# One more order of all steps on every queue of a linear-attention kernel chained with a GELU MLP

## The chip, the core and the metric

The kernel runs on one core of a Trainium2 chip. A core has a matrix engine (PE, with its weight loads shown apart as PEld), a vector engine (DVE), a scalar engine (ACT), a general engine (POOL) and a queue processor that issues transfers (SP). Each engine takes its own instructions strictly in order and waits for others by semaphores. The metric is the device time of one launch in microseconds (us); lower is better.

## The reference

The first part is a recurrent linear attention (RWKV7) with batch 4, 8 heads, 768 time steps and head size 40. For each head a 40 x 40 state is carried through time:

```python
for t in range(S):
    y[:, :, t] = np.einsum('bhd,bhde->bhe', rt, state)
    Sa = np.einsum('bhde,bhe->bhd', state, at)
    state_decay = state * wt[:, :, None, :] - np.einsum('bhd,bhe->bhde', Sa, bt)
    state = state_decay + np.einsum('bhd,bhe->bhde', vt, kt)
```

Its output, as 3072 tokens of 320 values, goes through an MLP with exact GELU:

```python
x = attn_out.transpose(0, 2, 1, 3).reshape(B * S, H * D)
h = x @ w_in                                     # 320 -> 2048
g = 0.5 * h * (1.0 + erf(h * inv_sqrt2))
return (g @ w_out).astype(np.float32)            # 2048 -> 320
```

All inputs are float32 except the two MLP weights, which come as float64 and are brought to float32 on the chip.

## The kernel before

The time axis is cut into 12 chunks of 64 steps. Inside a chunk the recurrence becomes a set of small matrix products with decays, plus the inverse of a triangular 64 x 64 matrix per head and batch; only the 40 x 40 state passes from chunk to chunk. When a chunk's output is there, its 256 tokens go through the MLP while later chunks are worked on.

The whole program is a list of 1450 small steps, written out as text in `order()` and run one after the other by `perform()`. A token such as `mh.1.0` calls the step `mh` with the numbers 1 and 0. The first number is the chunk for nearly all steps. Engines run what they are given in the order in which the tokens stand, so the text is the order of every queue. There is nothing else that decides it: no planner runs. Results of PE go to four PSUM banks, handed out round robin as they become idle (`take`, `drop`).

The steps that the following text names, with the engine in brackets:

- Loads (SP): `Lw`, `La`, `Lb`, `Lk`, `Lr`, `LV`, `Lv`, `Lwt`, `Lbt`, `Lkt` bring the inputs of one chunk; `Lf`, `Lf5` (L537) bring pieces of w_in and `Ls` (L577) of w_out.
- Conversion of the float64 weights: `ce`, `cn`, `cl` (ACT), `cs`, `cm`, `cv` (DVE) and `cg` (POOL, L658), in 18 units.
- Fillers (PE): `warm_first` and `warm.4.i` are matmuls whose result nobody uses. `warm_set` and `Tt_zero` are memsets.
- Decays: `lg` (ACT, a logarithm, L685), `wT` and `cu` (PE, products with a triangle of ones), `ew`, `ec` (ACT, L742); from chunk 3 on `tw` (PE), `lt` (ACT, logarithm), `pw`, `en`.
- Transposes: `ta`, `tb`, `tk`, `tr`, `tv` (PE), each followed by a scaled copy: `sa`, `sb` (DVE, L784), `sn`, `kc`, `rc`, `vc` (ACT).
- Products and masks: `nm` (PE), `nk` (DVE, L864); `am`, `ak`; `vm`, `vk`.
- The triangular inverse: for chunk 0 on PE and DVE (`qt`, `qi`, `qm` on PE, `qz` L1036, `qb` L1045, `qa`, `qc`, `ql`, `qx`); for the others on POOL (`ic.c.j0.j1`, L961 and L963), between `iz`, `nd`, `nx` (L927) and `wx`, `wa`, `wb`, `tc_`, `jm`, `jc`, `km`, `kt0`, `kt1`.
- Output and state: `av`, `xm`, `sm`, `pk`, `pb` (PE), `ym` (PE) and `yc` (ACT), `sc` (DVE, two passes of L1175, masks), `xc0`, `xc1`, `oa` and `om` (DVE, L1227, L1233), `od`, `oc`, `ot`, `tn`. `om` writes the tokens into `xt`.
- `ox.c.x` (SP, L1245 and L1248) moves part of `xt` to other partitions of SBUF by transfers, eleven for a chunk. The MLP's first product needs them.
- The MLP: `mh.c.p` (PE, L1307, 20 matmul records in 64x128 tiles), `ge.c.q` (ACT, GELU, L1312, for two `mh` each), then the second product in seven products of quarter size, `m1` to `m7` (PE, L1346), with the sums `s1` to `s4` before them and `e1` to `e6` after them (DVE L1299, ACT). Chunk 0 has a plain second product `pm.0.n` (PE, L1428) with copies `pc`. `so` and `sz` (SP) write the output.

ACT holds one set of function tables at a time; logarithm, exponential and GELU need different ones, so a change among them brings a table load.

Of the kernel before, what the change touches and what calls it, by code (L numbers as in the profile page):

```python
# [18 lines left out]
def order(chunks, first_seven):  # L19
    return """  # L20
        first_ones.1 Lw.1 stripes_set identity pads_extra.1 sums_mask Lw.0 pads_r.1 warm.4.20 upper_mask
        pads_extra.3 La.0 pads_a.1 warm.4.0 pads_VR.1 pads_VR.0 of_half_set Lb.0 bias_set warm.4.13 pads_r.0 lg.1
# [13 lines left out]
        mh.0.0 nk.2 ot.0.1 cg.6 ot.0.0 ak.1 Ls.1 nd.2 Ls.0 nx.2 mh.0.1 iz.2 ce.8 tn.0 LV.2 unused.a mh.0.2 wb.1
        cs.8 ic.2.0.4 Lk.2 cm.8 cv.8 ge.0.0 av.1 Ls.6 ce.11 ym.1 ce.10 cs.11 ic.2.4.8 Ls.5 mh.0.3 tc_.1 Lr.2
        cm.11 yc.1 sk.2.v xm.1 cs.10 Ls.7 ge.0.1 cm.10 tv.2 ic.2.8.12 Ls.9 xc1.1 cv.10 xc0.1 Ls.10 jm.1 vc.2
        cv.11 Ls.8 tr.2 ce.12 tk.2 Ls.11 mh.0.6 ce.13 cs.12 ic.2.12.16 La.3 cm.12 kc.2 cs.13 mh.0.7 wa.1.1 cm.13
        jc.1 cv.12 rc.2 am.2 vm.2 cv.13 ic.2.16.20 ce.14 pm.0.0 Ls.13 cl.14 cs.14 Ls.12 ce.15 cm.14 ak.2 Lw.3  # L40
# [5 lines left out]
        La.4 sa.3 wa.2.1 kt1.2 wa.2.0 nm.3 kt0.2 so.0.0 sm.2 nk.3 Lkt.3 mh.1.1 nd.3 sc.2.0 nx.3 lg.4 Lv.3 pk.2
        sc.2.1 ic.3.0.4 pb.2 ge.1.0 tk.3 mh.1.6 ic.3.4.8 oa.2.0 Lr.4 ta.4 mh.1.7 ws.0 LV.3 ws.1 mh.1.4 ge.1.3
        Lbt.4 ic.3.8.12 tr.4 mh.1.5 oa.2.1 Lk.4 kc.3 mh.1.2 tv.3 od.2.0 Lwt.4 ic.3.12.16 mh.1.3 od.2.1 oc.2
        om.2.0 vm.3 Lb.3 ge.1.1 am.3 ge.1.2 vk.3 m1.1 ot.2.1 ic.3.16.20 s1.1 ot.2.0 om.2.1 m2.1 s2.1 ox.2.1 ak.3
        m5.1 e1.1 tn.2 ws.3 av.3 e3.1 ic.3.20.24 s3.1 Lkt.4 ym.3 e2.1 tw.4 m6.1 yc.3 s4.1 ox.2.0 m3.1 ws.2 lt.4  # L50
        tk.4 m7.1 ic.3.24.28 e4.1 LV.4 tb.4 m4.1 e5.1 Lr.5 ic.3.28.31 xm.3 e6.1 pw.4 so.1.1 mh.2.6 xc0.3 La.5
        wx.3 ew.4 tc_.3 cu.4 sb.3 jm.3 en.4 so.1.0 mh.2.7 wb.3 sn.4 Lv.4 wa.3.0 jc.3 xc1.3 wa.3.1 km.3 sa.4 ec.4
        mh.2.4 sk.4.p tr.5 ge.2.3 kt1.3 Lkt.5 iz.4 ta.5 kt0.3 nm.4 sm.3 nk.4 Lw.5 mh.2.5 nd.4 nx.4 sc.3.0
        ic.4.0.4 mh.2.2 sc.3.1 Lbt.5 tv.4 mh.2.3 ic.4.4.8 kc.4 Lb.4 pk.3 ge.2.1 Lwt.5 ge.2.2 tb.5 pb.3 mh.2.0
        ic.4.8.12 sb.4 oa.3.1 oa.3.0 mh.2.1 od.3.0 om.3.1 am.4 ge.2.0 ic.4.12.16 om.3.0 vm.4 od.3.1 ox.3.1 m1.2
        s1.2 lg.5 tw.5 oc.3 ot.3.0 m2.2 s2.2 s4.2 m5.2 Lv.5 e1.2 vk.4 lt.5 ic.4.16.20 ot.3.1 s3.2 m6.2 ox.3.0
        ak.4 pw.5 m3.2 e3.2 ew.5 m7.2 La.6 e2.2 ic.4.20.24 tn.3 en.5 e4.2 m4.2 e5.2 av.4 e6.2 tk.5 so.2.1
        ic.4.24.28 ym.4 sn.5 Lr.6 mh.3.6 yc.4 sa.5 tv.5 LV.5 xm.4 ic.4.28.31 cu.5 xc1.4 xc0.4 mh.3.7 ec.5 wx.4
        tc_.4 wa.4.1 iz.5 ta.6 nm.5 ge.3.3 vm.5 Lbt.6 tr.6 wb.4 jm.4 nk.5 mh.3.2 jc.4 nd.5 Lwt.6 wa.4.0 nx.5
        mh.3.3 kc.5 ic.5.0.4 Lkt.6 vk.5 km.4 ge.3.1 mh.3.0 kt1.4 ic.5.4.8 kt0.4 tb.6 La.7 am.5 sm.4 tw.6  # L60
# [5 lines left out]
        ic.6.0.4 ge.4.3 jm.5 am.6 jc.5 wa.5.1 km.5 wa.5.0 tw.7 sk.5.p mh.4.3 kt0.5 tb.7 ic.6.4.8 kt1.5 La.8
        mh.4.0 ak.6 ge.4.1 sm.5 Lb.6 ic.6.8.12 mh.4.1 sc.5.1 tr.7 pk.5 sc.5.0 ge.4.0 Lkt.7 ic.6.12.16 pb.5 lt.7
        cu.6 oa.5.1 Lw.7 mh.4.4 oa.5.0 pw.7 ic.6.16.20 mh.4.5 LV.7 om.5.1 m1.4 ge.4.2 Lv.7 od.5.0 om.5.0 s1.4
        m2.4 ec.6 ox.5.1 s2.4 ic.6.20.24 m5.4 od.5.1 ew.7 s3.4 en.7 s4.4 m6.4 oc.5 sn.7 ot.5.0 so.3.0 ot.5.1 m3.4
        sa.7 Lk.7 nm.7 e1.4 ox.5.0 ic.6.24.28 e3.4 e2.4 m7.4 e4.4 tn.5 m4.4 e5.4 ic.6.28.31 av.6 e6.4 nk.7 so.4.1  # L70
        sk.6.p ym.6 sb.6 wx.6 mh.5.6 wb.6 tv.7 iz.7 nd.7 tk.7 yc.6 mh.5.7 nx.7 Lr.8 wa.6.1 ic.7.0.4 vm.7 ge.5.3
        xm.6 Lwt.8 vk.7 mh.5.2 ic.7.4.8 xc0.6 ta.8 kc.7 Lbt.8 mh.5.3 xc1.6 tc_.6 tr.8 mh.5.0 ic.7.8.12 ge.5.1
        Lkt.8 tb.8 jm.6 lg.7 am.7 jc.6 Lb.7 wa.6.0 km.6 ic.7.12.16 tw.8 mh.5.1 so.4.0 kt1.6 ak.7 kt0.6 lt.8 Lv.8
        mh.5.4 pw.8 ic.7.16.20 ge.5.0 sm.6 mh.5.5 sc.6.0 sc.6.1 pk.6 ge.5.2 s1.5 pb.6 Lk.8 cu.7 oa.6.1 m1.5 La.9
        om.6.1 oa.6.0 ec.7 m2.5 sk.7.p od.6.0 om.6.0 s2.5 ox.6.1 m5.5 ic.7.20.24 e1.5 od.6.1 s3.5 oc.6 ew.8 m6.5
        s4.5 en.8 e2.5 m3.5 LV.8 e3.5 ot.6.0 e4.5 sa.8 ot.6.1 ox.6.0 m7.5 tn.6 ic.7.24.28 tk.8 m4.5 e5.5 Lr.9
        ic.7.28.31 av.7 e6.5 sb.7 sn.8 ym.7 so.5.1 mh.6.2 yc.7 wx.7 tc_.7 iz.8 Lb.8 xm.7 nm.8 mh.6.3 nk.8 nd.8
        tv.8 mh.6.6 xc1.7 Lwt.9 ge.6.1 nx.8 mh.6.7 kc.8 ic.8.0.4 Lw.8 vm.8 ge.6.3 am.8 xc0.7 vk.8 jm.7 ic.8.4.8
        wa.7.1 tw.9 mh.6.4 ta.9 lt.9 Lv.9 jc.7 pw.9 wb.7 mh.6.0 ic.8.8.12 lg.8 Lbt.9 wa.7.0 km.7 mh.6.1 kt1.7
        ak.8 kt0.7 ic.8.12.16 sm.7 ge.6.0 mh.6.5 sc.7.1 sc.7.0 tb.9 cu.8 ge.6.2 ic.8.16.20 Lw.9 pk.7 s1.6 pb.7  # L80
# [1386 lines left out]
```

## Time and profile before

| | us |
|---|---|
| median of three runs | 639.3 (638.05 to 640.16) |
| the profiled execution, its span | 638.6 |
| PE busy | 621.4 |
| PEld busy | 548.3 |
| DVE busy | 457.9 |
| POOL busy | 380.3 |
| ACT busy | 323.6 |

The profiled execution took its span; no other time lies around it. In the rows of the timeline the first number is the start in us, the second the length of the stretch, then the engine and the line; the tile written stands left of the arrow, the tiles read right of it; x8 counts instructions, and what released the first of them after idle time stands in brackets. "SPq" is the stretch in which SP issues a transfer, not its landing. Rows by windows give the busy time of each engine in that window with the number of instructions, then the clock granted to PE, the share of the DMA engines and GB/s. The chain of waits is followed back from the last instruction; its rows have start, length, engine and line.

### The profile page before, as it was taken

What the parts mean: (1) busy time and instruction counts of PE and PEld (TensorE: products, weight loads), DVE (VectorE), ACT (ScalarE), POOL (GpSimd) and SP (SyncE); (2) the same over time, 40 slices, a digit from 0 to 9 for tenths busy, and PEclk for the clock granted to TensorE, in tenths of its full rate; (3) what the DMA queues carried; (4) which work ended last, traced back from release to release, by engine and by line L of the source; (5) the groups of instructions that cost most, each with busy time, mean ns of one, the idle gap of its engine ahead of it and who ended that gap; (6) DMA issues with size and microseconds to landing.
All of it is one profiled execution on the core that took longest, in us unless ns stands there. A gap on an engine that the chain in (4) does not pass through costs nothing.

```text
span 638.6 us, 27896 instructions
## 1 busy us (share of the span) xinstructions
PE 621.4 (97%) x12418; PEld 548.3 (86%) x12418; DVE 457.9 (72%) x557; ACT 323.6 (51%) x456; POOL 380.3 (60%) x782
## 2 busy tenths in 40 slices
...
PEclk9799999999999999999999999999999999999999
...
GB/s 136 181 162 178 91 178 187 143 104 137 91 135 149 59 98 159 64 147 111 110 84 133 76 93 107 88 88 157 68 92 109 41 37 84 42 26 3 36 7 21
DMA packets 246899, 64.07 MB, mean 100 GB/s; under 512 B 228380, under 2 KB 243644, under 8 KB 246780
## 3 DMA queue, kind: packets, MB, share of 16 engines
...
q14 instruction: 22, 0.18, 0.1%
...
## 4 chain that ended last, share of the span: by engine, by line
PE 76%; ACT 2%; DVE 0%; issue 0%; DVEq 0%
PE bank L1307 30%; PE bank L1346 27%; PE bank L193 19%; ACT Tt L937 0%; ACT SM L1154 0%; ACT L1312 0%; ACT spare L922 0%; DVE spare L864 0%; ACT st L1194 0%; ACT gt L1312 0%; ACT T L942 0%; DVE Tt L932 0%; ACT st L1192 0%; ACT Tt L1116 0%; DVE os L1299 0%
## 5 line engine op out<-in xcount | busy, mean ns | idle before, releaser
L1307 PE MATMUL bank<-xt,w_in_sb 64*128 64x256 f32 x1920 | 221.3, 381 | 0.2 <-ACT gt L1312 0.2
L961 POOL TENSOR_TENSOR tmp<-W,Nb 128x126 f32<-128x126 f32 (+22 forms) x341 | 164.4, 482 | 93.1 <-DVE Nb L927 67.6
L1307 PEld LDWEIGHTS bank<-xt,w_in_sb 64*128 64x128 f32 x1920 | 182.5, 187 | 25.1 <-issue 1.5
L963 POOL TENSOR_TENSOR W<-W,tmp 128x126 f32<-128x126 f32 (+22 forms) x341 | 168.8, 495 | 26.7
L1346 PE MATMUL bank<-w_out_sb,gt 128*128 128x160 f32 x704 | 101.1, 301 | 0.0
L1346 PEld LDWEIGHTS bank<-w_out_sb,gt 128*128 128x128 f32 x704 | 96.6, 190 | 2.2 <-issue 1.2
L1312 ACT ACTIVATE gt<-bank 128x1024 f32<-128x1024 f32 x48 | 48.7, 1024 | 94.9 <-PE bank L1307 94.6
L1175 DVE TENSOR_TENSOR SM<-bank,upper 128x832 f32<-128x832 f32 (+1 forms) x24 | 23.0, 988 | 20.3 <-PE bank L193 20.2
L1263 ACT COPY conv<-st 32x128 f32<-32x128 f32 (+2 forms) x55 | 28.0, 509 | 17.0 <-DVE st L1257 16.2
L1299 DVE TENSOR_TENSOR conv<-gt 128x1024 f32<-128x1024 f32 x11 | 14.2, 1290 | 25.1 <-ACT gt L1312 25.0
L1227 DVE TENSOR_TENSOR st<-bank,st 128x832 f32<-128x832 f32 (+1 forms) x22 | 21.2, 985 | 14.0 <-PE bank L193 14.0
L1346 PE MATMUL bank<-extra,conv 128*128 128x160 f32 x208 | 30.3, 300 | 0.0
L1299 DVE TENSOR_TENSOR os<-os,bank 128x160 f32<-128x160 f32 x44 | 13.8, 315 | 22.1 <-PE bank L1346 20.5
L1346 PEld LDWEIGHTS bank<-extra,conv 128*128 128x128 f32 x208 | 28.9, 190 | 0.1
L721 DVE TENSOR_TENSOR_SCAN kT<-spare,kT 128x256 f32<-128x256 f32 x36 | 26.6, 798 | 0.6 <-ACT kT L714 0.6
L1346 PE MATMUL bank<-extra,gt 128*128 128x160 f32 x176 | 25.8, 300 | 0.0
L1346 PEld LDWEIGHTS bank<-extra,gt 128*128 128x128 f32 x176 | 24.5, 190 | 0.1
L789 POOL TENSOR_TENSOR bk_rows<-bk_rows,part 128x640 f32<-128x640 f32 x9 | 14.3, 1591 | 14.3 <-ACT part L742 13.9
L1312 ACT ACT_TABLE_LOAD x17 | 21.8, 1283 | 0.3
L1346 PE MATMUL bank<-extra,SM 128*128 128x160 f32 x144 | 21.2, 300 | 0.0
L193 PEld LDWEIGHTS bank<-SM,Tt 64*64 64x64 f32 x768 | 17.1, 133 | 4.2 <-issue 2.3
L193 PE MATMUL bank<-SM,Tt 64*64 64x104 f32 (+1 forms) x768 | 19.3, 249 | 0.9 <-ACT Tt L1113 0.9
...
## 6 DMA issues: line engine op xcount, KB each, us to landing
...
```

What stands on the lines that cost most here:

```text
L193: nc.tensor.matmul(o, lhsT, rhs, start=first, stop=True, skip_group_check=True)
L721: nc.vector.tensor_tensor_scan(logs[:, at:at + n], onward, logs[:, at:at + n], 0.0, ALU.mult, ALU.add)
L789: (nc.vector if q == "v" else nc.gpsimd).tensor_tensor(to, rows(k_of(c)), decays(c), ALU.mult)
L961: nc.gpsimd.tensor_tensor(t, W[:, BL // 2 - rows:, rest:rest + 1].to_broadcast([P, rows, rest]), Nb[:, rest:rest + 1, :rest].to_broadcast( ...
L963: nc.gpsimd.tensor_tensor(own, own, t, ALU.add)
L1175: nc.vector.tensor_tensor(SM[:, g, :, :, cols], pair_of(f"S{c}_", g).rearrange("p x i c -> p i x c")[:, :, :, cols], kept, ALU.mult)
L1227: nc.vector.tensor_tensor(to, pair_of(f"QY{c}_", g)[:, :, :, cols], to, ALU.add)
L1263: nc.scalar.copy(apart.rearrange("p e i g d -> p (e i g) d")[to_rows, :, to_col:to_col + n], st.rearrange("p e i g c -> p (e i g) c")[rows ...
L1299: nc.vector.tensor_tensor(to, one_, other, how)
L1307: nc.tensor.matmul(ph[:, x, s], w_in_sb[half(x), kt, p * P:(p + 1) * P], xt[half(x), kt], start=kt == 0, stop=kt == NK - 1)
L1312: nc.scalar.activation(gt[:, 4 * q:4 * q + 4].rearrange("p (x s) t -> p x s t", x=2), bank(f"ph{c}_{q}").rearrange("p x (s t) -> p x s t", ...
L1346: nc.tensor.matmul(po[:, n, :DM // 2], l_[:, f], r_[:, f], start=f == 0, stop=f == NF // 2 - 1)
```

## The change

Only the text in `order()` is changed. The list holds the same 1450 tokens, each as often as before, in another order; after it every line number is smaller by five, since the text is five lines shorter. Instructions, tiles, sizes and buffers are the same, except that the PSUM bank of a product depends on the order, and that table loads of ACT go where the order puts them: 55 of them after, 48 before.

The beginning, before and after (chunk 0's loads and `warm_first` first; chunk 1's steps later):

```diff
-        first_ones.1 Lw.1 stripes_set identity pads_extra.1 sums_mask Lw.0 pads_r.1 warm.4.20 upper_mask
-        pads_extra.3 La.0 pads_a.1 warm.4.0 pads_VR.1 pads_VR.0 of_half_set Lb.0 bias_set warm.4.13 pads_r.0 lg.1
-        first_ones.0 pads_w.0 pads_rows.0 warm.4.25 pads_extra.0 Lb.1 pads_rows.1 onward_set lg.0 pads_w.1 wT.1
-        pads_a.0 pads_extra.2 La.1 wT.0 warm.4.2 ew.1 Lf.0.1.0 ta.0 Lf.1.1.0 cu.0 Lf.0.0.0 cu.1 ec.0 Lf.1.0.0
-        ew.0 sb.0 tb.0 sa.0 Lk.0 warm.4.15 sn.0 ec.1 nm.0 sb.1 Lf.2.0.0 warm_set tb.1 nk.0 Lf5.0.0 ta.1 sn.1 qt
-        parity_set iz.1 sa.1 qm.0 qi.0.p qi.1.v nm.1 qz.0 warm_first ce.1 Lf.3.0.0 nk.1 qb.0.0.v Lf.3.1.0 qc.0
-        cs.1 qb.0.1.a nd.1 qm.1 sk.0.p ce.0 nx.1 Lr.0 cm.1 Tt_zero tk.0 cs.0 cn.1 ic.1.0.4 qc.1 Lf.2.1.0 cl.1
...
+        Lw.0 pads_a.1 warm_set pads_a.0 Tt_zero identity bias_set pads_VR.1 warm_first sums_mask warm.4.25 La.0 Lb.0
+        pads_extra.3 lg.0 of_half_set pads_w.0 warm.4.13 wT.0 upper_mask first_ones.0 cu.0 pads_extra.0 ec.0 sb.0 ta.0
+        Lw.1 ew.0 sa.0 tb.0 sn.0 nm.0 stripes_set parity_set nk.0 qt warm.4.24 lg.1 Lf.1.0.0 Lf.1.1.0 qi.0.p ce.1 cs.1
+        cm.1 pads_extra.1 cu.1 Lb.1 La.1 qm.0 qz.0 qb.0.0.v ec.1 pads_w.1 wT.1 ew.1 cn.1 sb.1 pads_extra.2 ta.1 tb.1
+        sn.1 first_ones.1 sa.1 qb.0.1.a qc.0 nm.1 qi.1.v qm.1 cl.1 nk.1 Lk.0 Lf.2.1.1 qz.1 qb.1.0.v warm.4.0 Lf.0.0.0
```

From the first `om` to the first `mh`, and around the second `pm` pair:

```diff
-        La.2 tv.1 om.0.1 om.0.0 Ls.2 cs.4 cm.4 Lf.3.0.1 vc.1 tr.1 od.0.1 cv.4 ox.0.0 am.1 rc.1 unused.v wT.2 ce.6
-        sb.2 warm.4.1 one_set od.0.0 wx.1 ew.2 ta.2 ox.0.1 tb.2 sa.2 vm.1 sn.2 cs.6 cl.6 cm.6 nm.2 vk.1 oc.0 cn.6
...
-        cv.16 pk.1 cn.17 cg.17 pb.1 ge.0.2 oa.1.0 cu.3 Lk.3 oa.1.1 pm.0.3 ec.3 od.1.0 Lw.4 ic.2.28.31 od.1.1 oc.1
-        tw.3 ot.1.0 om.1.1 sk.3.p ot.1.1 om.1.0 av.2 tn.1 ox.1.1 pc.0.1 lt.3 ym.2 wx.2 iz.3 pm.0.2 tc_.2 yc.2
...
+        cl.6 od.0.1 vc.1 Lb.2 sb.2 wT.2 oc.0 ot.0.0 warm.4.20 La.2 ta.2 Lk.2 cs.4 cm.4 tb.2 Ls.0 ic.1.24.28 ic.1.28.31
+        ox.0.0 ew.2 cv.4 unused.a sa.2 vm.1 sn.2 Ls.2 Lf.3.1.1 ox.0.1 wx.1 warm.4.4 ce.6 ot.0.1 cs.6 cm.6 cn.6 nm.2
...
+        ce.17 cm.16 ak.2 pk.1 pb.1 lg.3 cs.17 cm.17 cn.17 ic.2.20.24 Lwt.3 mh.0.4 mh.0.5 tw.3 lt.3 Lr.3 oa.1.0 LV.3
+        od.1.0 cv.16 oa.1.1 od.1.1 ge.0.2 Lbt.3 cu.3 cg.17 Lb.3 Lv.3 om.1.1 om.1.0 ox.1.0 ec.3 pm.0.3 av.2 ic.2.24.28
```

One later place, around the products of chunk 4:

```diff
-        kt1.4 ic.5.4.8 kt0.4 tb.6 La.7 am.5 sm.4 tw.6
-        ic.5.8.12 mh.3.1 lt.6 Lk.5 sc.4.1 sc.4.0 Lw.6 ak.5 mh.3.4 ge.3.0 pw.6 ic.5.12.16 mh.3.5 Lv.6 pk.4 ge.3.2
-        s1.3 pb.4 so.2.0 lg.6 av.5 oa.4.1 ic.5.16.20 oa.4.0 m1.3 od.4.1 od.4.0 om.4.0 oc.4 m2.3 om.4.1 ot.4.0
...
+        mh.3.5 wa.4.0 kt0.4 ge.3.2 tr.6 sm.4 sc.4.0 Lkt.6 Lv.6 sc.4.1 pk.4 pb.4 s1.3 oa.4.0 od.4.0 oa.4.1 od.4.1 m1.3
+        oc.4 ot.4.1 s2.3 om.4.1 m2.3 e1.3 ic.5.8.12 m5.3 av.5 ot.4.0 ic.5.12.16 ic.5.16.20 ic.5.20.24 om.4.0 tn.4 ym.5
```

The rest of the list is reordered in the same manner; within the blocks of the MLP the `mh` steps and `m` steps stand in longer runs at some places and in shorter ones at others.

More of the change, by code (lines that the diff above doesn't have):

```diff
@@ L36, in order @@
[L36 to L40, printed above, removed]
@@ L46, in order @@
[L46 to L50, printed above, removed]
@@ L51, in order @@
[L51 to L60, printed above, removed]
@@ L66, in order @@
[L66 to L75, printed above, removed]
@@ L76, in order @@
[L76 to L80, printed above, removed]
@@ new lines, in order @@
+        tb.3 oc.1 ot.1.0 ot.1.1 tn.1 ym.2 pm.0.2 yc.2 ic.2.28.31 pw.3 wx.2 tc_.2 ew.3 sa.3 en.3 jm.2 jc.2 wa.2.0
+        wa.2.1 xm.2 xc0.2 sn.3 unused.r tr.3 ox.1.1 nm.3 nk.3 Lkt.3 pc.0.1 sb.3 mh.1.0 wb.2 nd.3 nx.3 km.2 kt1.2 xc1.2
+        mh.1.1 pc.0.0 kt0.2 sm.2 tv.3 La.4 ge.1.0 sc.2.1 sc.2.0 vm.3 vk.3 tk.3 kc.3 Lr.4 ta.4 Lbt.4 Lk.4 mh.1.2 pk.2
+        pb.2 mh.1.4 mh.1.5 oa.2.1 od.2.1 ge.1.2 mh.1.6 mh.1.7 ge.1.3 oa.2.0 od.2.0 ws.0 ws.1 ws.2 mh.1.3 tr.4 oc.2
+        so.0.0 ot.2.1 am.3 om.2.0 Lk.3 ge.1.1 m1.1 Lw.4 m2.1 ak.3 av.3 ot.2.0 tn.2 ym.3 om.2.1 Lwt.4 ox.2.0 e1.1 s1.1
@@ new lines, in order @@
+        mh.2.1 od.3.0 am.4 om.3.1 Lwt.5 Lr.5 tw.5 so.1.1 so.1.0 La.6 vm.4 om.3.0 ge.2.0 s1.2 s4.2 Lv.5 s2.2 m1.2 m2.2
+        s3.2 m5.2 m6.2 lt.5 iz.4 e1.2 e2.2 m3.2 m7.2 ic.4.0.4 ak.4 m4.2 vk.4 e3.2 ic.4.4.8 ic.4.8.12 ic.4.12.16
+        ic.4.16.20 ic.4.20.24 pw.5 ox.3.1 e4.2 e5.2 oc.3 ot.3.0 ox.3.0 ot.3.1 tn.3 ew.5 Lk.5 e6.2 so.2.1 cu.5 ec.5
+        av.4 en.5 tr.5 ym.4 tv.5 sn.5 mh.3.6 yc.4 mh.3.7 ge.3.3 Lkt.5 sa.5 tk.5 kc.5 ic.4.24.28 xm.4 xc1.4 ta.6 Lw.6
+        xc0.4 nm.5 nk.5 ic.4.28.31 wx.4 tc_.4 nd.5 nx.5 Lwt.6 iz.5 mh.3.2 mh.3.3 ge.3.1 LV.5 ic.5.0.4 am.5 vm.5 mh.3.0
```

104 lines of the change are left out of this document (63 added, 41 removed).

## The prediction

> **What bounds the kernel now.** I read the page's busy times first, then busy time by windows of 20 us, then the chain of waits, then the queues line by line over the first 140 us.
>
> ```profile
> span 638.6 us, 27896 instructions
> PE 621.4 (97%) x12418; PEld 548.3 (86%) x12418; DVE 457.9 (72%) x557; ACT 323.6 (51%) x456; POOL 380.3 (60%) x782
> PE 76%; ACT 2%; DVE 0%; issue 0%; DVEq 0%
> ...
> 20.00:40.00 20.00, 16.99 (x352) 11.77 (x350) 15.82 (x23) 11.39 (x17) 12.78 (x25) 0.83 1.07 167
> 40.00:60.00 20.00, 17.40 (x502) 13.66 (x504) 19.30 (x30) 15.15 (x23) 17.27 (x35) 1.00 0.85 173
> 60.00:80.00 20.00, 19.50 (x542) 16.78 (x544) 17.47 (x30) 15.47 (x22) 6.81 (x14) 1.00 0.59 108
> 120.00:140.00 20.00, 17.12 (x406) 12.89 (x400) 15.08 (x21) 16.94 (x24) 7.49 (x12) 1.00 0.46 89
> ...
> 138.94:635.03 496.09, 495.34 (x9590) 451.29 (x9584) 351.79 (x402) 224.08 (x323) 293.77 (x590) 1.00 0.47 86
> ```
>
> PE works 97% of the span, and 76% of the chain of waits lies on it. In a window columns follow as PE, PEld, DVE, ACT, POOL, then PEclk. From 138.94 us to the last matmul PE is busy for 495.34 of 496.09 us, and no other engine is full. So an order can win there only by removing small stalls or changes of tile form. The holes are in the head: 3.01, 2.60 and 2.88 us in three of the four early windows shown. At 40 to 60 us it is DVE that is full, 19.30 of 20.
>
> **The head.** Part 1, chunk 0's loads and first chain come ahead of chunk 1's.
>
> ```profile
> 0.81 1.48 SPq L447 DMA_DIRECT2D SM<-in_w_dram  x2
> 2.32 1.94 SPq L447 DMA_DIRECT2D w_tile<-in_w_dram  x2
> 2.70 6.26 PE L193 MATMUL bank<-cum_m,ident 128*128 128x512 f32 x8 [2.70 <-POOL cum_m L360]
> 9.87 1.11 PE L193 MATMUL bank<-cum_m,w_tile 64*64 64x64 f32 x64
> 12.75 1.24 PE L193 MATMUL bank<-w_tile,cum_m 128*128 128x320 f32 x4
> 19.72 1.16 DVE L864 TENSOR_TENSOR N<-bank,upper 128x1024 f32<-128x1024 f32 x1
> ```
>
> The two Lw.1 transfers (1.48 us of SP) leave the way of Lw.0, La.0 and Lb.0, and wT.1, ta.0 and a filler leave the way of cu.0 on PE. Four fillers ended at 2.70 + 6.26 = 8.96; now warm_first and two fillers stand there, started by DVE's short memset instead of POOL's cum_m. I let them end near 8.2 (estimate: warm_first's 4.86, row below, from about 1, and half of the 6.26 shortened as the clock rises). wT.0 (1.11) follows, then cu.0 at about 9.3 instead of 12.75. From cu.0 to nk.0 it was 19.72 - 12.75 = 6.97, so nk.0 comes at about 16.3: 3.4 earlier.
>
> Part 2, warm_first leaves the inverse of chunk 0.
>
> ```profile
> 27.69 4.86 PE L193 MATMUL bank<-w_in_sb 128*128 128x512 f32 x6
> 28.97 0.48 DVE L1045 TENSOR_SCALAR st<-st,of_half 128x512 f32<-128x512 f32 x1
> 32.48 2.08 PE L193 MATMUL bank<-turned,st 64*64 64x64 f32 x64
> ...
> 20.88:67.83 46.95, 40.95 (x1066) 31.15 (x1066) 41.72 (x64) 31.75 (x45) 33.40 (x68) 0.93 0.97 169
> ...
> 66.54 1.29 DVE L1233 TENSOR_TENSOR xt<-bank,wpT 128x512 f32<-128x512 f32 x2 [0.15 <-PE bank L193]
> ```
>
> qm.1's last input was there at 28.97 + 0.48 = 29.45, but PE sat in warm_first until 32.5. That is 3.0 more, 6.4 with part 1. ACT takes ec.1 and ew.1 ahead of chunk 0's copies now, so I take 5.6: qm.1 near 26.9. Not all of this lasts. From nk.0's end to om.0's end DVE is busy for 41.72 of 46.95 us, and in the new order it has nearly the same passes there; kc.0 and other copies on ACT stand between too. That gives back about 1.6 (estimate; at worst 5.6, with om.0 where it was, at best nothing). I put om.0 at 66.54 - 4.0.
>
> Part 3, SP's queue.
>
> ```profile
> 64.52 1.33 SPq L577 DMA_DIRECT2D w_out_sb<-in_moe_w_out_dram  x2
> 65.91 0.61 SPq L537 DMA_DIRECT2D gt<-in_moe_w_in_dram  x1
> 67.91 0.90 SPq L1245 DMA_DIRECT2D xt<-xt  x1
> 74.34 3.25 SPq L1248 DMA_DIRECT2D xt<-xt  x4
> 76.58 7.27 PE L1307 MATMUL bank<-xt,w_in_sb 64*128 64x256 f32 x60
> 78.83 4.61 PEld L1307 LDWEIGHTS bank<-xt,w_in_sb 64*128 64x128 f32 x42 [0.23 <-DMA xt<-xt]
> ```
>
> The first MLP product waits for the eleven transfers of ox.0.0 and ox.0.1, which SP issues one after the other from 67.91 to 77.59. After the change Ls.2 (1.33) and Lf.3.1.1 (0.61) stand between the two: 1.9 of the 4.0 are given back. mh.0.0 gains 2.0 to 2.6.
>
> Part 4, from there to mh.1.0, the last piece of the head.
>
> ```profile
> 119.85 1.56 POOL L658 TENSOR_TENSOR conv<-conv,bk_rows 128x640 f32<-128x640 f32 x1 [1.00 <-ACT conv L650]
> 122.16 0.77 PE L193 MATMUL bank<-w_tile,cum_m 64*64 64x320 f32 x8 [1.36 <-ACT gt L1312]
> 122.86 4.58 PE L1428 MATMUL bank<-w_out_sb,gt 128*128 128x320 f32 x16
> 138.25 0.22 PE L193 MATMUL bank<-Tt,Js 32*32 32x32 f32 x2 [1.52 <-ACT Js L1091]
> 138.94 2.43 PE L1307 MATMUL bank<-xt,w_in_sb 64*128 64x256 f32 x20
> ```
>
> Stalls of 1.36 and 1.52 stand here, and both go: the instructions in front are others. New ones come. ge.0.2 on ACT stands behind lt.3, so behind tw.3 on PE and the load Lwt.3 on SP; and on SP, Lb.3 waits for POOL's cg.17 (at 119.85), with Lv.3, ox.1.0 and ox.1.1 queued behind it. pm.0.3, which needs ge.0.2, may then stand still for up to 3 us, and jm.2 and nm.3 for some tenths. nm.3 comes before mh.1.0 now and km.2 after it, which I let cancel. Bounds for mh.1.0's gain: 2.6 + 1.36 + 1.52 = 5.5 with no new stall; 2.0 + 2.9 - 3.0 - 1.0 = 0.9 with all of them. I take half of a 2.6 us stall: 2.3 + 2.9 - 1.3 = 3.9.
>
> **The steady part.** The same 1450 steps are issued, so PE's matmuls are the same. What can differ is the changes between tile forms and stalls.
>
> ```profile
> 184.46 2.36 PE bank L1307 x20
> 602.15 17.47 PE bank L1307 x160
> ```
>
> A single mh step (20 matmuls) takes 2.36; eight in a row 17.47/8 = 2.18. One interruption costs 0.18, or less where the neighbour has another form. Counted over both PE queues from mh.1.0 on there are 130 runs of one form before, 135 after; weighed by form this adds 0.66 us (bounds: 0, and 5 x 0.2 = 1.0).
>
> ```profile
> 435.01 1.66 PE L193 MATMUL bank<-SM,Tt 64*64 64x104 f32 x64
> 436.49 0.72 PE L193 MATMUL bank<-w_tile,cum_m 64*64 64x320 f32 x8
> 436.63 1.02 DVE L1175 TENSOR_TENSOR SM<-bank,upper 128x832 f32<-128x832 f32 x1 [1.85 <-PE bank L193]
> 465.76 0.32 DVE L1299 TENSOR_TENSOR os<-os,bank 128x160 f32<-128x160 f32 x1
> ```
>
> The kernel of before keeps small work between a product and the step that reads its mask. pb needs both sc passes of 1.02 behind sm, 2.04 and a handover (0.1, as an estimate). In chunks 4 and 10 the new order has sm, pk, pb adjacent, so only pk's 1.66 lies in front: 2.04 + 0.1 - 1.66, about 0.5 each. av.7 and av.8 stand behind the passes of e5 (0.32 each) with two short steps between, 0.3 each; m1.1 behind ge.1.1 (1.02), 0.45; ym.10 and mh.9.4 0.5 together; the rest, by the same subtraction, 0.9 (all estimates). Sum 3.5. In before the window above shows 0.75 of open idle time, and PE takes 2.2 more than its matmuls at the rates of unbroken runs, such as 2.18 above; I count the 2.2. So +1.3; bounds -2.2, with no stall at all, and +5, if each handover is 0.2 longer in some 20 places.
>
> ACT loads its function tables 55 times instead of 48.
>
> ```profile
> L1312 ACT ACT_TABLE_LOAD x17 | 21.8, 1283 | 0.3
> L1312 ACT ACTIVATE gt<-bank 128x1024 f32<-128x1024 f32 x48 | 48.7, 1024 | 94.9 <-PE bank L1307 94.6
> ```
>
> Seven more are 7 x 1.28 = 9.0 us of an engine that is busy half the time. I take 0, since ge, which releases PSUM banks, waited 94.6 us for PE and not the other way; the bound is 9.0, all on the path. [...]
>
> **The tail.** e5.11, its output, e6.11 and the last output stay in that order; 0.
>
> ```profile
> 635.07 0.32 DVE L1299 TENSOR_TENSOR os<-os,bank 128x160 f32<-128x160 f32 x1 [0.91 <-PE bank L1346]
> ```
>
> **Sum.** 638.6 - 3.9 + 0.66 + 1.3 = 636.7 for a profiled execution. The profile of before lies 0.7 under the median of its runs (639.3; 638.05 to 640.16), hence 637.4 less rounding: I forecast 637.3.
>
> **The rivals.** *The head's gain stays whole.* If ge.0.2 and ox.1 come in time, mh.1.0 gains 5.5, and if the tight places cost no more than before the steady part adds 0.66: 639.3 - 4.8 = 634.5. For it: the stalls at 122.16 and 138.25 are real and their cause is gone. Against: SP's order gives back 1.9 in sight, and the sums at pb.4 and pb.10 leave little room.
>
> *Slower: Gelu behind a table switch.* The new order puts ge.0.2, ge.2.2, ge.2.0, ge.4.1, ge.6.1, ge.7.3 and ge.8.0 directly behind a switch, after steps that themselves wait for PE (lt, lg, ec). There are four PSUM banks, so a late ge holds its bank and PE's next product waits. Each exposed switch costs 1.28, all seven 9.0: 637.4 + 9.0 = 646.4, with four of them 642.5. The change is slower than before from the second exposed one on (1.9/1.28 = 1.5). For it: PE is without a gap, so no delay is absorbed later. Against: ge waits for PE in before by 94.6 us in 48 calls, 2 each.
>
> *No change: the clock.*
>
> ```profile
> PEclk9799999999999999999999999999999999999999
> ```
>
> PEclk is 7 in the second slice and 0.83 at 20 to 40; it fell while PE ran the small tiles of the inverse, and warm_first filled that stretch. If qm.1 to qm.3 now run at half clock, their 2.08 each doubles, plus transposes and products around them: about +6 in the chain up to om.0, the 4.0 are lost and 2 more, while the old stalls of 2.9 still go: 639.3 + 2.0 - 2.9 + 0.66 + 1.3 = 640.4. Against: qm steps are short and DVE is the bound at 40 to 60. [...]
>
> **How the numbers follow.** Small net gain (637.3, own range 635.8 to 639) 0.43; whole gain 0.22; Gelu behind switches 0.25; clock 0.10. Differences under 0.3% (637.4 to 641.2) a measurement of this kernel can't tell from no change. Of the first case a little over half lies below 637.4, all of the second: faster 0.46. The upper end of the third and a few executions of the first lie above 641.2, with unseen stalls of the same kind: slower 0.30. Same 0.24. Range 632.5 to 644: below, the whole gain with the -2.2 of no stalls at all; above, five exposed switches.
>
> **What would show it.** nk.0 at 16 to 17 and qm.1 at 26 to 27.5 show parts 1 and 2; the time between the transfers of ox.0.0 and of ox.0.1 shows part 3; pm.0.3's idle time and mh.1.0 at 134 to 136 show part 4. From mh.1.0 to the last matmul I expect 498.1 instead of 496.1. Idle time of PE put down to "ACT gt L1312" above 3 us would show the slower rival; PEclk under 0.8 at 20 to 40 the clock. The prediction is wrong if PE's idle time after 140 us is far from 3.5 us in total, either way.

## The result, and the profile after

The changed kernel takes 647.7 us (median of 4 executions, 646.4 to 650.1) against 638.9 for the kernel before (4 executions in the same session): ratio 1.0135, 95% interval 1.0103 to 1.0166. It is slower, where a small gain was forecast, and longer than the 632.5 to 644 that the forecast allowed. One correction to the table above: in these runs the time of an execution is its span plus 1.9 us (646.81 for the changed kernel's profiled one, span 644.9). So the profile of before stands for about 640.5, a little above its median and not 0.7 under it. The forecast used the difference only.

Three lines of the changed kernel's page:

```profile
span 644.9 us, 27921 instructions
PE 625.9 (97%) x12418; PEld 551.6 (86%) x12418; DVE 457.7 (71%) x557; ACT 332.5 (52%) x463; POOL 375.0 (58%) x782
PEclk9798989999999999999999999999999999999999
```

and its busy time by windows, columns as before:

```profile
20.00:40.00 20.00, 16.25 (x286) 13.24 (x281) 11.80 (x18) 10.42 (x15) 7.04 (x17) 0.74 0.98 182
40.00:60.00 20.00, 17.84 (x491) 14.36 (x483) 17.56 (x28) 15.07 (x22) 17.41 (x35) 0.91 0.85 160
80.00:100.00 20.00, 19.20 (x384) 16.67 (x384) 14.63 (x23) 14.81 (x20) 16.37 (x37) 0.91 0.89 203
...
141.33:641.28 499.95, 497.05 (x9588) 450.53 (x9584) 350.61 (x403) 232.57 (x329) 289.64 (x593) 1.00 0.47 86
```

The clock falls three times ahead of the last matmul where it fell once: the trace's clock records have half clock from 22.6 to 32.8, 53.3 to 56.7 and 80.6 to 84.0 us (before: 24.95 to 31.78 only). mh.1.0 starts at 141.33 instead of 138.94, 2.4 later where 3.9 earlier was forecast. From there to the last matmul it takes 499.95 instead of 496.09, 3.9 more where 2.0 was forecast. That is the 6.3 us between the two profiles.

The head line by line, first PE, then DVE, then SP:

```profile
18.11 1.42 PE L188 MATMUL bank<-N,st 32*32 32x32 f32 x128 [0.40 <-DVE st L995]
23.19 0.49 PE L188 MATMUL bank<-cum_m,SM 64*64 64x64 f32 x7 [2.65 <-issue]
23.61 1.97 PE L746 MATMUL bank<-ident,spare 128*128 128x128 f32 x8
25.36 1.91 PE L746 MATMUL bank<-ident,extra 128*128 128x128 f32 x8
28.38 1.99 PE L188 MATMUL bank<-aT,nT 40*64 40x64 f32 x64 [1.10 <-DVE turned L1002]
30.14 3.24 PE L188 MATMUL bank<-turned,st 64*64 64x64 f32 x64
51.92 0.57 PE L188 MATMUL bank<-rT,late 40*64 40x64 f32 x21 [1.17 <-issue]
80.80 6.16 PE L1302 MATMUL bank<-xt,w_in_sb 64*128 64x256 f32 x38 [1.70 <-DMA xt<-xt]
126.60 4.54 PE L1423 MATMUL bank<-w_out_sb,gt 128*128 128x320 f32 x16 [0.50 <-issue]
...
15.55 1.23 DVE L859 TENSOR_TENSOR N<-bank,upper 128x1024 f32<-128x1024 f32 x1 [2.02 <-PE bank L188]
68.04 1.27 DVE L1228 TENSOR_TENSOR xt<-bank,wpT 128x512 f32<-128x512 f32 x2
...
69.38 0.91 SPq L1240 DMA_DIRECT2D xt<-xt  x1
73.83 0.91 SPq L572 DMA_DIRECT2D w_out_sb<-in_moe_w_out_dram  x2
74.78 0.78 SPq L532 DMA_DIRECT2D gt<-in_moe_w_in_dram  x2
75.61 1.57 SPq L1240 DMA_DIRECT2D xt<-xt  x2
```

nk.0 (15.55) does come 4.2 us earlier. But PE then stands still for 2.65 us inside wT.1, put down to "issue": nothing in the profile that it waits for. The clock falls there, and ta.1 and tb.1 (1.97 and 1.91, where the old order took 1.04 and 1.09) and most of qm.1 (3.24 instead of 2.08) run at half clock; nm.1 (1.99) did so in the kernel before as well. om.0 (68.04) comes 1.5 later than before, not 4 earlier.

The rows show one thing more. wT.1, ta.1 and tb.1 ran ahead of qm.0 in the old order; now they stand between qm.0 and qm.1, in the place that warm_first has left. With the pause, and the wait at nm.1, PE goes from the end of qm.0 (19.53) to qm.1 in 10.6 us, where it took 6.6. The queue of ACT waits for them, too:

```profile
23.73 1.04 ACT L723 ACTIVATE wpT<-bank 128x1024 f32<-128x1024 f32 x1 [4.08 <-PE bank L188]
27.32 1.01 ACT L796 COPY nT<-bank 128x1024 f32<-128x1024 f32 x1 [2.04 <-PE bank L746]
28.85 0.57 ACT L1026 COPY turned<-bank 128x512 f32<-128x512 f32 x1
```

ew.1 (23.73) waits for wT.1 and sn.1 (27.32) for tb.1, and qc.0 (28.85), the last step that qm.1 needs, stands behind both. It ends at 29.42. In the kernel before, qm.1's last input was there at 29.45. So the whole gain of part 1 is gone before qm.1 begins.

**What the pauses under "issue" are.** The page has a queue "q8 instruction" with 97 transfers, 1.59 MB, so 16 KB each; PE executes 12418 matmuls and as many weight loads, and 1.59 MB over these is 64 bytes each. So I read q8 as PE's stream of instructions: 128 matmul records, with their loads, to a transfer (an estimate from these counts). From the records of the trace, the pauses inside one step of small tiles in four kernels (records counted from the first matmul; us):

```
kernel      step   record  transfer starts, lands   PE goes on   behind the landing
before      qm.0      348      22.25    23.72          25.30          1.58
changed     wT.1      350      20.47    21.56          23.19          1.63
changed     vm.0      858      49.14    50.27          51.92          1.66
h_after     vm.0      858      50.54    52.02          53.62          1.60
fill_three  qm.1      476      28.35    29.31          30.81          1.50
changed     ym.6     6592     326.85   328.24         329.73          1.49
changed     xm.8     8758     430.85   431.88         433.25          1.37
```

In these rows PE goes on 1.4 to 1.7 us behind a landing, and within the head the places lie 126 records (350 to 476) or four times 127 (350 to 858) apart. The transfers of q8 start at least 3.34 us apart in the profile of the kernel before and 3.60 in that of the changed one, while 128 records of small tiles run in 1.4 to 3.3 us (in the changed kernel the 128 of qm.0 in 1.4, 64 of nm.0 in 1.2, 64 of sm.4 in 1.66). So, as I read these numbers, a long run of small tiles uses up its instructions here; no experiment tests that alone. What sets the start of a transfer isn't shown.

Past mh.1.0 the view of PE's waits (total, times, longest), and then two rows of the timeline with the places under "issue":

```profile
PE bank L188 <- issue: 1.3, 2, 0.8
PE bank L1302 <- DVE os L1294: 0.7, 1, 0.7
PE bank L188 <- DVE SM L1170: 0.5, 2, 0.4
```

```profile
329.72 0.91 PE L188 MATMUL bank<-rT,turned 40*64 40x64 f32 x43 [0.49 <-issue]
433.25 0.58 PE L188 MATMUL bank<-st,aT 40*64 40x104 f32 x13 [0.78 <-issue]
```

Against each step's own usual length in these kernels, the largest excesses are xm.8 1.3, mh.2.6 0.9 (the next mh needs a bank that DVE's sums release), ym.6 0.8, pb.4 0.8, pb.10 0.5, ym.10 0.3, av.7 0.2, am.9 0.2. No wait of PE for GELU ("ACT gt") is left.

### The profile page after: what moved, and what is told of

Read it like the earlier page. It is cut to its first block, busy times and chain, and to the rows that moved or that the text cites. A ratio compares the mean times of both kernels' runs of the same rounds, so it can differ in the third digit from the quotient of the medians.

```text
span 644.9 us, 27921 instructions
## 1 busy us (share of the span) xinstructions
PE 625.9 (97%) x12418; PEld 551.6 (86%) x12418; DVE 457.7 (71%) x557; ACT 332.5 (52%) x463; POOL 375.0 (58%) x782
## 3 DMA queue, kind: packets, MB, share of 16 engines
q8 instruction: 97, 1.59, 1.1%
## 4 chain that ended last, share of the span: by engine, by line
PE 91%; DVE 4%; issue 2%; SPq 1%; DMA 1%; ACT 1%; DVEq 0%; ACTq 0%
PE bank L1302 34%; PE bank L188 28%; PE bank L1341 25%; PE bank L1423 3%; DVE SM L1170 1%; PE bank L746 1%; DMA xt<-xt 1%; DVE kT L716 0%; SPq L1243 0%; DVE conv L630 0%; DVE turned L1002 0%; DVE xt L1228 0%; ACT L729 0%; DVE st L995 0%; DVE spare L859 0%
## 5 line engine op out<-in xcount | busy, mean ns | idle before, releaser
L1302 PE MATMUL bank<-xt,w_in_sb 64*128 64x256 f32 x1920 | 224.6, 384 | 2.8 <-DMA xt<-xt 1.7
L956 POOL TENSOR_TENSOR tmp<-W,Nb 128x126 f32<-128x126 f32 (+22 forms) x341 | 165.9, 486 | 74.6 <-DVE Nb L922 49.1
L958 POOL TENSOR_TENSOR W<-W,tmp 128x126 f32<-128x126 f32 (+22 forms) x341 | 162.2, 476 | 26.7
L941 POOL MEMSET W<- 128x512 f32 x11 | 5.8, 524 | 50.3 <-DVE Tt L927 50.3
L1149 DVE COPY SM<-bank 128x832 f32<-128x832 f32 (+1 forms) x10 | 9.8, 981 | 16.7 <-PE bank L188 16.7
```

What stands on the lines that cost most here:

```text
L956: nc.gpsimd.tensor_tensor(t, W[:, BL // 2 - rows:, rest:rest + 1].to_broadcast([P, rows, rest]), Nb[:, rest:rest + 1, :rest].to_broadcast( ...
L958: nc.gpsimd.tensor_tensor(own, own, t, ALU.add)
L1302: nc.tensor.matmul(ph[:, x, s], w_in_sb[half(x), kt, p * P:(p + 1) * P], xt[half(x), kt], start=kt == 0, stop=kt == NK - 1)
```

## The experiments

Each time is a median, beside the kernel before on the same chip (640.2; for lean, lean_old, b_lean and b_short 640.7). "Old" and "new" name the two orders.

**Which part costs.** h_before and h_after are spliced at mh.1.0.

```diff
 h_before: [old order up to mh.1.0] + [new order of all other steps]
 h_after:  [new order up to mh.1.0] + [old order of all other steps]
```

> The steps that the kernel of before has ahead of mh.1.0, in its order, then all others in the new order. The profiles put the loss in two places: mh.1.0 comes 2.4 us later, and from there to the last matmul it takes 3.9 us more. Theory A (the loss is the sum of two parts that don't depend on each other): about 639 + 3.9 = 643, and PE's idle time past 145 us like that of the new kernel (pb.4, pb.10, mh.2.2). Rival (all of the 8.8 us comes from the head and its clock): within 0.3% of before, 637 to 641.

> The steps that the new kernel has ahead of mh.1.0, in its order, then all others in the order of before. Theory A: mh.1.0 near 141 as in the new kernel, granted clock under 0.9 somewhere in the first 100 us, time about 639 + 2.4 to + 5 (the runs of the new kernel lie 2 us above its profile, which can be the clock falling otherwise in other executions): 641 to 644. Rival (the loss is in the steady part): 637 to 640.

Measured: 649.5 (ratio 1.0136, 1.0105 to 1.0167) and 646.5 (1.0090, 1.0059 to 1.0122), both above everything that was expected. The steady windows of h_after and h_before:

```profile
144.37:640.06 495.69, 495.14 (x9524) 450.63 (x9520) 348.74 (x398) 221.98 (x319) 295.61 (x594) 1.00 0.46 86
```
```profile
143.50:644.01 500.51, 498.46 (x9524) 452.64 (x9520) 348.63 (x399) 231.68 (x327) 288.76 (x590) 1.00 0.46 84
```

Each part loses by itself. The steady part keeps its length whatever the head is: 495.7 to 497.7 us in the eight profiles with the old order (a ninth, b_swap, moves mh.1.0 itself), 499.9 to 502.7 in the seven with the new one left as it is. (The windows of the two splices hold 64 records fewer, those of nm.3 or km.2, about 1 us.) The times don't add so simply, because each splice has a seam. At h_after's, km.2 comes ahead of mh.1.0 besides nm.3: nm.3 starts 0.5 later than in the changed kernel (140.75 beside 140.26, with pauses in vm.0 of 2.8 and 1.2 us), mh.1.0 3.0 later (144.4 beside 141.3). At h_before's, nm.3 and its neighbours come ahead of mh.1.0, 4.5 us.

**SP's queue.**

```diff
- ox.0.0 ... Ls.2 Lf.3.1.1 ox.0.1
+ ox.0.0 ... ox.0.1 Ls.2 Lf.3.1.1
```

> The new kernel with Ls.2 and Lf.3.1.1 issued behind ox.0.1 instead of between ox.0.0 and ox.0.1. Part 3 of the prediction: ox.0.1 is issued 1.7 to 1.9 us earlier, PE's idle time of 1.7 us inside mh.0.0 and the half clock behind it (80 to 84 us) go, mh.0.1 comes 3 to 5 us earlier than in the new kernel, and mh.1.0 1 to 4 earlier: 644 to 646.5. Rival (the head is bound by something later, pm.0.3's GELU or the weights' conversion): mh.0.1 earlier, mh.1.0 and the time unchanged, 647 to 648.5.

Measured: 649.9 (1.0136, 1.0102 to 1.0170), above both ranges, though the ratio is that of the changed kernel (1.0135). The rows of ACT and PE, from the longest of its six executions:

```profile
90.06 0.75 ACT L605 ACTIVATE conv<-gt,rebias 128x512 int16<-128x512 int16 x1 [7.44 <-DMA gt<-in_moe_w_in_dram]
```
```profile
93.84 5.36 PE L1301 MATMUL bank<-xt,w_in_sb 64*128 64x256 f32 x24 [4.60 <-ACT gt L1306]
```

ce.8 on ACT waits for Lf.3.1.1, ge.0.0 stands behind ce.8, and mh.0.2 waits for ge.0.0. mh.0.1 starts 0.6 us earlier than in the changed kernel (83.80), mh.0.2 4.4 later. So moving the two loads behind ox.0.1 gains nothing.

**Fillers and the clock.**

```diff
 warm_back  (new): - warm_first at the start   + warm_first behind wT.1
 warm_early (old): - warm_first behind qz.0    + warm_set warm_first at the start
 fill_one   (new): + three fillers (128x512) behind qm.0
 fill_three (new): as fill_one, + one before vm.0, + two before mh.0.0
 fill_old:  [head of fill_three up to mh.1.0] + [old order of all other steps]
```

> The new kernel with warm_first (three wide filler matmuls, 4.8 us at half clock) behind wT.1, where PE comes out of a pause of 2.9 us at half clock, instead of at the very start. Clock theory: solid work brings the full clock back near 28 us instead of 32.8, qm.1 to qm.2 run at full clock, and the 4.8 us cost less than 1.5 net at qm.2 (which was at 37.9): the time between -2 and +1.5 us of the new kernel. Rival (the clock matters little, the chain of chunk 0 does): qm.2 4 us later and the time 3 to 5 us longer.

> The kernel of before with one part of the change alone: warm_set and warm_first at the very start instead of between qm.0 and qm.1. [...] Part 2 of the prediction (warm_first only stands in the way of qm.1): qm.1 near 29.6, qm.2 near 34.5, time 636.5 to 638.

> The new kernel with three more fillers (128x512, 1.0 us each) behind qm.0, where PE pauses for 2.65 us and the clock halves from 22.6 to 32.8 us. Clock theory: no pause there or one under 1 us, no half clock before 40 us, nm.1 and qm.1 at full clock, qm.2 at 33.5 to 36 instead of 37.9, and the time 1.5 to 4 us below the new kernel's, 643.5 to 646. Rival (the chain of chunk 0 on DVE and ACT sets qm.2, the clock matters little): qm.2 between 37 and 39, the time 647 to 649.

> As fill_one, with one more filler before vm.0 (a pause of 1.2 us and half clock from 53.3 to 56.7) and two before mh.0.0 (a pause of 1.7 us for the transfers of ox, half clock from 80.6 to 84.0). Clock theory: no half clock in the first 120 us, mh.0.1 between 78 and 81 instead of 84.4, the time 2 to 4 us below fill_one. Rival: the pauses only move, half clock somewhere else in the first 100 us, and the time like fill_one's.

> The head of fill_three up to mh.1.0, then all other steps in the order of before. The steady part of the new order costs 3.9 us more from mh.1.0 to the end in the profile, that of before -0.4 behind the new head: so 3 to 5 us below fill_three if both theories hold, and at or below the kernel of before, 635 to 640. Rival (the head's loss isn't the clock): 644 to 648 as h_after.

Measured:

| | us | ratio | qm.2 | mh.1.0 | half clock in the head |
|---|---|---|---|---|---|
| warm_back | 652.6 | 1.0185 (1.0158 to 1.0211) | 42.6 | 145.7 | 23.4 to 30.2, 57.5 to 64.3 |
| warm_early | 641.3 | 1.0011 (0.9982 to 1.0040) | 37.0 | 141.5 | 24.9 to 35.2, 55.6 to 62.5, at 141 |
| fill_one | 648.2 | 1.0136 (1.0094 to 1.0178) | 36.7 | 140.5 | 49.1 to 56.0, 79.9 to 83.3 |
| fill_three | 647.4 | 1.0125 (1.0095 to 1.0156) | 36.4 | 138.9 | 57.0 to 60.4 |
| fill_old | 645.8 | 1.0111 (1.0066 to 1.0157) | 38.1 | 143.6 | 32.1 to 35.5, 56.0 to 59.4 |

warm_early is the plainest. In its profiled execution, the longest of ten, qm.1 starts at 29.73, as part 2 has it. But the old head, too, has 10.2 us of half clock now instead of 6.8, qm.1 takes 3.68 instead of 2.08, and qm.2 gains 0.4 instead of the 3 that part 2 counted. The median time is that of the kernel before.

```profile
20.00:40.00 20.00, 15.39 (x349) 12.67 (x346) 16.05 (x24) 11.91 (x18) 12.67 (x24) 0.74 1.00 175
```
```profile
29.73 3.68 PE L187 MATMUL bank<-turned,st 64*64 64x64 f32 x64 [1.83 <-DVE st L1039]
```

warm_back speaks for the rival: the full clock was back at 30.2 us, 2.6 earlier, yet qm.2 came 4.8 later and the ratio rose from 1.0135 to 1.0185, some 3 us: warm_first stands in the chain there for 5.49 us. Three fillers behind qm.0 did take the half clock at 22 to 33 away, and fill_three most of the rest: mh.1.0 2.5 earlier than in the changed kernel. The time did not follow (the intervals of fill_one, fill_three and the changed kernel overlap; fill_three's steady part is 502.0), so the half clock of the head isn't shown to be what the change cost. fill_old, put at 635 to 640, took 645.8: with the same steps ahead of it as in fill_three nm.3 starts 3.0 later there (140.76 beside 137.79), and the seam takes another 1.7. And with the clock nearly whole, fill_three's mh.0.0 is still later than before (79.89 beside 76.58). Its rounds of the inverse show where some of it goes:

```profile
28.24 1.26 PE L188 MATMUL bank<-turned,st 64*64 64x64 f32 x34
30.81 1.14 PE L188 MATMUL bank<-turned,st 64*64 64x64 f32 x30 [1.31 <-issue]
31.88 1.13 PE L188 MATMUL bank<-cum_m,ident 128*128 128x512 f32 x2
32.85 1.04 PE L746 MATMUL bank<-ident,extra 128*128 128x128 f32 x8
33.72 1.02 PE L188 MATMUL bank<-conv,ident 128*128 128x512 f32 x2
34.58 1.06 PE L188 MATMUL bank<-w_out_sb,ident 128*128 128x512 f32 x2
35.48 1.02 PE L188 MATMUL bank<-cum_m,ident 128*128 128x512 f32 x2
36.43 2.02 PE L188 MATMUL bank<-turned,st 64*64 64x64 f32 x61
```

From qm.1 (28.24) to qm.2 (36.43) PE is at work or paused all the time: a pause, warm.4.0, tk.0, cx.1 (two rows), warm.4.1. From qm.1 to qm.4 the new head takes 17.8 to 18.0 us in after, h_after, sp_free, fill_one and fill_three, the old one 14.4 in before, h_before, b_swap and b_fill.

**The rounds, and warm_first.**

```diff
 lean (new): + three fillers behind qm.0, + two before mh.0.0
-  warm.4.0 warm.4.1 warm.4.2
+  qc.1 qb.1.1.a ahead of kc.0
 lean_old: [head of lean up to mh.1.0] + [old order of all other steps]
 b_fill (old):  + two fillers ahead of qm.0
 b_lean (old):  as b_fill, - warm_first
 b_short (old): - warm_first
 b_swap (old):  mh.1.0 ahead of km.2
```

> The new kernel with the three fillers of fill_one behind qm.0 and two before mh.0.0, without the fillers warm.4.0, warm.4.1 and warm.4.2 that stand between the rounds qm.1 to qm.4, and with qc.1 and qb.1.1.a ahead of kc.0 on ACT. Order theory: qm.1 to qm.4 takes 14.5 to 15.5 us instead of 17.8, mh.1.0 comes 2 to 3 us earlier than in fill_three, 136 to 137.5, and the time is 644 to 646. Rival (pauses for instructions set it): the fillers' time turns into pauses or half clock, qm.1 to qm.4 17 us or more, 647 to 649.

> The head of lean up to mh.1.0, then the order of before. If head and steady part add: 640 to 642.5, the steady part 496 to 497.5. Rival (a mixture at the seam loses 3 us more, as fill_old did): 643 to 646.

> The kernel of before with two more fillers (1.0 us each) ahead of qm.0, so that PE isn't idle ahead of its pause for instructions at 25.3. Clock theory: no half clock at 25 to 32 us, warm_first takes 2.5 instead of 4.86, qm.1 1 to 2.3 us earlier and the time 0.5 to 2 us shorter, 638 to 639.5. Rival (DVE sets the chain there): qm.2 within 0.7 of before and no change of the time, 639.5 to 641.5.

> b_fill (the kernel of before with two fillers ahead of qm.0) without warm_first. If the whole clock behind the two fillers is enough, qm.1 comes when its inputs are there, 0.5 to 1.5 us earlier than in b_fill, and the time is 637.5 to 639. Rival (warm_first is still needed behind the pause in qm.0): half clock from 25 or 28 us on, 640 to 642.

> The kernel of before without warm_first, and no filler in its place. Clock theory: half clock from 25 us for 10 us or more on qm.1 and its neighbours; 640.5 to 643. Part 2 of the prediction (warm_first only stands in the way): qm.1 at 29.5, 637 to 638.5.

> The kernel of before with mh.1.0 ahead of km.2, so that PE works while jc.2 on ACT ends (a stall of 1.52 at 138.25). If the stall is local: mh.1.0 1.5 us earlier, time 638 to 639.5 beside 640. Rival (mh.1.0 waits for ox.1 or for a bank just as long): no change, 639.5 to 641.

b_lean and b_short leave warm_first out, whose result nobody uses. Measured: lean 646.7 (1.0112, 1.0064 to 1.0161), qm.1 to qm.4 16.9 us, but 10.2 us of half clock from 46.4 on, and mh.1.0 at 138.4. Of the 3.4 us that the new order costs there, only 1.0 went with the fillers and the earlier copies. In their place PE pauses, and waits for copies by ACT:

```profile
30.30 1.14 PE L187 MATMUL bank<-turned,st 64*64 64x64 f32 x30 [1.04 <-issue]
34.86 2.02 PE L187 MATMUL bank<-turned,st 64*64 64x64 f32 x61 [0.63 <-ACT st L1037]
44.88 2.25 PE L187 MATMUL bank<-turned,st 64*64 64x32 f32 x61 [1.85 <-ACT st L1037]
```

lean_old took 643.6 (1.0056, 1.0031 to 1.0081). b_lean took 640.1 (0.9984, 0.9964 to 1.0004), with half clock from 26.4 to 33.3, behind a pause of 2.2 us in qm.0. b_short took 641.2 (1.0007, 0.9986 to 1.0029): without warm_first the time stays the same, so it costs about as much as it gives. b_swap took 640.0 (0.9998, 0.9980 to 1.0016): mh.1.0 now waits 1.08 for its transfers, nm.3 0.41 for DVE and sm.2 0.44 for ACT. **b_fill takes 639.0, ratio 0.9979 (0.9963 to 0.9994), the only one whose interval lies below the kernel before.** Of its page two lines, of its timeline PE around qm.0, and its window from mh.1.0 to the last matmul:

```profile
span 635.1 us, 27904 instructions
PEclk9999999999999999999999999999999999999999
```

```profile
20.62 1.88 PE L187 MATMUL bank<-cum_m,ident 128*128 128x512 f32 x4
22.43 1.05 PE L187 MATMUL bank<-N,st 32*32 32x32 f32 x100
24.82 0.44 PE L187 MATMUL bank<-N,st 32*32 32x32 f32 x28 [1.33 <-issue]
25.19 1.16 PE L187 MATMUL bank<-aT,nT 40*64 40x64 f32 x64
26.28 2.84 PE L187 MATMUL bank<-w_in_sb 128*128 128x512 f32 x6
29.05 2.11 PE L187 MATMUL bank<-turned,st 64*64 64x64 f32 x64
```

```profile
135.35:631.51 496.16, 495.52 (x9592) 451.28 (x9584) 352.63 (x402) 224.03 (x323) 292.39 (x590) 1.00 0.47 87
```

The fillers (20.62) fill PE's idle time ahead of qm.0, the pause remains (1.33) but is short, the clock stays whole, and warm_first takes 2.84 instead of 4.86: qm.1 at 29.05 instead of 32.48. These 3.4 us reach the end of the span (635.1 against 638.6). Not every execution has that luck: in 12 executions of b_fill the four with a granted clock of 1.000 took 636.4 to 637.4 us, the four with 0.997 (some 4 us at half clock) 639.0 to 639.7. The median gains 1.2 us. Executions of the kernel before at 0.997 took 638.0 to 639.2 on the same chip, so at the same clock b_fill is no faster: it gains where the clock stays whole.

**Mending the steady part.** Five steps moved a little at the largest stalls.

```diff
 mend_steady (new): mh.2.7 ahead of mh.2.2, m1.3 ahead of pb.4, m1.9 ahead of pb.10,
                    mh.7.4 ahead of xm.8, mh.5.6 ahead of ym.6
 mend_all: as mend_steady, with the fillers of fill_three
```

> The new kernel with five steps moved a little, one at each of the largest stalls past mh.1.0 that its profile and those of its variants share: mh.2.7 ahead of mh.2.2 (0.7 to 0.9 us, bank released by DVE), m1.3 ahead of pb.4 (0.8) and m1.9 ahead of pb.10 (0.5, both behind the sc passes), mh.5.6 ahead of ym.6 (0.8) and mh.7.4 ahead of xm.8 (1.3; in both PE pauses for a block of its instructions in a run of small tiles). Theory: each stall was local, PE is the bound, so the steady part shrinks from 500 by 2.5 to 4.3, less 0.2 for each new border of forms, and the time by 2 to 3.5 us to 644 to 646. Rival (the stalls only absorb what DVE, POOL or the blocks impose anyway): they come back at the next steps, steady part 499.5 to 502, time 647 to 649.

> mend_steady with the six added fillers of fill_three in the head. If head and steady part add, mh.1.0 stands at 138 to 141 and the steady part at 497 to 499: 641 to 645. Rival (what the head gains is lost past it again, as fill_three's steady part of 502 suggests): 646 to 648.

In both, mh.5.6 stands ahead of ox.5.1, so part of its product is made from the tokens of the chunk before, and ox.5.1 has to wait for it. These two kernels compute something else, then, and they test the idea only in part. Measured: 653.5 (1.0211, 1.0184 to 1.0238) and 648.5 (1.0129, 1.0097 to 1.0161), with steady parts of 506.4 and 507.6: longer, not shorter. Stalls came back next door: jm.3 waits 0.6 where mh.2.2 did, ym.5 waits 1.4 for a transpose by DVE (tn.4), and mh.5.7 waits 1.2 for the transfers of the ox.5.1 that mh.5.6 held up. That the steady part's loss can be mended step by step isn't shown.

## Why the prediction was wrong, point by point

- **Part 1 (nk.0 3.4 earlier): right.** It came 4.2 earlier.
- **Part 2 (warm_first out of the way, qm.1 5.6 and om.0 4.0 earlier): this is the step that failed.** qm.1 came 2.3 earlier and om.0 1.5 later. Two terms of it failed. The first is the step from 6.4 to 5.6, the 0.8 that chunk 1's steps may cost: wT.1, ta.1 and tb.1 now stand between qm.0 and qm.1, PE pauses in wT.1 for 2.65 us, and qm.1's last input was there at 29.42 instead of 29.45, so all that part 1 gained was lost before qm.1. I had taken warm_first for a pure obstacle and had not asked what takes its place. In both kernels PE pauses near record 350, and warm_first was the work at half clock behind that pause; in the new order ta.1, tb.1 and qm.1 ran at half clock instead (in warm_early, qm.1). The second term is the "about 1.6" that is given back up to om.0: it was 3.8. The rounds from qm.1 to qm.4 alone cost 3.4 more. In the changed kernel 1.2 of it is qm.1 at half clock; fill_three and fill_one need as much at whole clock, and lean, without the fillers between the rounds and with qc.1 ahead of kc.0, saves 1.0 of it. The rest are pauses and copies that PE waits for; the share of each stays open.
- **Part 3 (1.9 given back on SP): right in size**, 73.83 to 75.61. What came behind it was not in the sum: PE waits 1.70 inside mh.0.0, the clock falls, and mh.0.0 takes 6.0 us (78.40 to 84.42) instead of 2.6.
- **Part 4 (old stalls go, up to 3 us at pm.0.3): right, and better than taken.** From mh.0.1 to mh.1.0 it took 56.9 instead of 59.8 us, as much less as the 1.36 + 1.52 of the old stalls; pm.0.3 waited 0.5.
- **Steady part (+2.0): right in direction, too small**, +3.9 in the profile. The stalls came nearly as summed: PE's idle time is 499.95 - 497.05 = 2.9 where 3.5 was forecast. The term that failed is the 2.2 that was taken off for the kernel before: PE's busy time did not shrink, it rose by 1.7. pb.4 (0.8), pb.10 (0.5), ym.10 (0.3) and av.7 (0.2) stalled about as summed. xm.8 and ym.6 (pauses under "issue", 0.78 and 0.49) and mh.2.2 (a bank that DVE releases) were not in the sum; the stalls named at m1.1 and av.8 didn't come. No run shows the 0.1 that the sum took for a handover: in the changed kernel pb.4 and pb.10 go on 0.05 behind the second sc pass (261.75 to 261.80, 548.15 to 548.21).
- **ACT's seven more table loads at 0: right, as far as the rows show.** Each of the 55 changes among logarithm, exponential and GELU brought one load of 1.28 us, as each of the 48 in the kernel before. ACT is busy 8.9 us longer, but PE has no wait for GELU left; that rival falls.
- **The clock rival named something that happened, at the right place, but its price was wrong.** Its sign came (PEclk 0.74 at 20 to 40). It put +6 on qm.1 to qm.3; only qm.1 ran at half clock (+1.2), with ta.1 and tb.1 (+1.8) ahead of it. It had one fall of the clock and an end at 640.4; there were three, the pauses behind two of them weren't seen as such, and the steady loss came on top. By fill_three the clock alone doesn't explain the time. The row that showed it stood in the timeline of before, and I had not read it as a pause that ends 1.58 us behind the landing of a transfer of q8:

```profile
25.30 0.54 PE L193 MATMUL bank<-N,st 32*32 32x32 f32 x24 [1.92 <-issue]
```

What stays open: how long a pause is in a given execution (1.2 and 2.8 us for vm.0 in two kernels with the same steps ahead of it), so how the 8.8 us of the medians split between head and steady part. Taking 500 to 502 against 496.5 for the steady part, some 4 to 5 of them lie there and 3 to 4 in the head (an estimate from the profiles). That the order of the steps past mh.1.0 costs this much is shown by the windows of fifteen profiles; which stalls make it up is read off one profile and not tested.
